# Last two row blocks of an attention and mixture-of-experts kernel: one due-time order for all operations, and W2's low parts by subtraction instead of an adding transfer

## The chip, the cores and the metric

One core of a Trainium2 chip runs the whole kernel. The metric is the device time of one execution in microseconds (us); the median of three runs of the kernel before is 937.79 us (935.74 to 939.01).

## The reference

Block-causal attention over 4 batches, 8 heads, 576 positions and 64 channels (mask block 64), and then a mixture of 4 experts whose weights are given row by row. All of it is float32.

```python
scores = scale * np.matmul(q, k.transpose(0, 1, 3, 2))       # masked where block_i < block_j
attn = softmax(scores)                                        # max, exp, sum
x = (attn @ v).transpose(0, 2, 1, 3).reshape(2304, 512)
p = domain_probs / (domain_probs.sum(-1, keepdims=True) + 1e-09)
for e in range(4):
    h = np.maximum(x @ w1[e], 0.0)                            # 512 -> 1024
    out += p[:, e:e+1] * (h @ w2[e])                          # 1024 -> 512
```

## The kernel before

**Precision.** TensorE gets every float32 operand as two parts: a high part, rounded by a copy to the type F32R, and a low part, the operand less its high part. A product is three matmuls (high by high, high by low, low by high). So each weight tile, each activation and each sum costs a copy (`a_copy`, line 407, ScalarE or VectorE, whichever would end first) and a subtraction (`tt` with SUB, line 413, VectorE) before TensorE can use it.

**Stages.** The 2304 rows are five blocks. Blocks 0, 1 and 2 go through the experts one at a time (`mm1`, `mm2`), beside the attention of the blocks that follow. The last 1024 rows, blocks 3 and 4, are taken together in `both_blocks` (line 1380), and there both layers use a scheme with 7 products of sub-blocks in place of 8 (Strassen's, in Winograd's form), which asks for sums and differences of sub-blocks of x, W1, h and W2, each split into parts again.

**The loop of `both_blocks`.** It runs over 16 pairs of F chunks, j = 0 to 15. A pair has 7 first-layer products (`product`, line 1588: 6 matmuls of 512 columns each). Between them stand second-layer units (`mm2_second`, line 1502: 3 matmuls of 256 columns each). Two pairs make a group g (7 groups); a group's 56 units run two pairs later, 28 in an even pair, by the shares `LATER[0] = [2, 4, 4, 4, 4, 5, 5]`, and 28 in the next, odd one, 4 after each product. TensorE's order is thus written out by hand. Within a group the units come by product x = 0 to 6 (the table `SECOND`: A11, S3, S2, A22, S1, A12, S4), each for the group's two pairs.

**What each group needs.** `w2_group` (line 1123), `w2_sums` (line 1137) and `w2_parts` (line 1151) make W2's parts: for each of the two pairs a quarter (x = 0, 256 columns) and three tiles of 512 columns (x = 1 to 3, two of them with sums of quarters). For x = 0 the low part is a VectorE subtraction. For x = 1 to 3 ScalarE writes the raw tile negated and rounded, which is minus the high part, into the low tile (line 1158), and GpSimd starts a transfer that adds the raw tile into it (`add_dma`, line 401). `h_group` (line 1427) and `h_parts` (line 1440) do the same split for h: 14 copies and 14 subtractions of 512 columns a group. `second_sums` (line 1450) makes the sums of h, `w_pair` (line 1100) those of W1, `snap` (line 1631) and `total` (line 1637) gather the first layer's products out of PSUM. `out_second` (line 1539) scales the finished second-layer tiles and, from the second group on, adds them to the output in DRAM by adding transfers of 128 KB on GpSimd's queue.

**Buffers.** Late in the kernel there are 6 tiles each for W2's high and low parts, 6 raw W2 tiles, 10 each for h's high and low parts, and 13 tiles `sc` for first-layer results and sums of h.

**What sets the order.** All of this is generated ahead of time by a planner, `Flow` (line 95). Every step is an `Op` with an engine, an estimated cost and a priority. `Flow.est` (line 135) estimates when each step could start; `Flow.run` (line 212) takes the earliest, and among the steps of the same engine that could start no later, the one with the lowest priority number. The result is a fixed instruction order on each engine; the engines work through it strictly in that order and wait for one another by semaphores. Before the change the priorities are fixed levels: 0.0 for what frees PSUM, 0.1 for sums of h, 0.2 or 0.4 for parts of h, 1.0 or 2.5 (5.0 when far off) for W1 and W2, 1.0 for output transfers. The planner also keeps GpSimd's steps, transfers among them, apart from VectorE's SBUF steps (`self.port`, lines 150 and 244).

Of the kernel before, what the change touches and what calls it, by code (L numbers as in the profile page):

```python
# [11 lines left out]
ALU = mybir.AluOpType  # L12
# [82 lines left out]
class Flow:  # L95
# [39 lines left out]
    def est(self, op):  # L135
        best = None
        for eng, cost in (op.eng if isinstance(op.eng, list) else [(op.eng, op.cost)]):
            t = self.clock[eng]
            for v in op.r:
                if v.t is None:  # L140
                    return None
                x = v.t + (self.SELF if v.eng == eng else self.LAT + op.lag + (self.SLACK if eng == "pe" else 0.0))
                if x > t:
                    t = x
            if op.bytes and len(self.landed) >= 8:
                t = max(t, self.landed[-8])
            for b in op.u:
                if b.base + self.LAT + op.lag / 2 > t:
                    t = b.base + self.LAT + op.lag / 2
            if eng == "pool":  # L150
                t = max(t, self.port)
            elif eng == "dve" and op.port:
                t = max(t, self.port)
                for a, b in self.held() if self.later else ():
                    if a - self.AHEAD < t < b:
                        t = b
            score = t + cost + self.bias.get(eng, 0.0) + (op.pen() if eng == "dve" else 0.0)
            if best is None or score < best[0]:
                best = (score, t, eng, cost)
        return best[1:]  # L160
# [51 lines left out]
    def run(self):  # L212
        while self.threads:
            k = 0
            while k < len(self.threads):
                th = self.threads[k]
                if self.advance(th):
                    k += 1
                else:
                    self.threads.pop(k)  # L220
            if not self.threads:
                break
            cands = []
            for th in self.threads:
                if isinstance(th[1], Op):
                    e = self.est(th[1])
                    if e is not None:
                        cands.append((e, th))
            assert cands, "stuck"
            first = min(cands, key=lambda c: (c[0][0], c[1][1].prio()))  # L230
            eng = first[0][1]
            near = [c for c in cands if c[0][1] == eng and c[0][0] <= first[0][0]]
            (t, eng, cost), th = min(near, key=lambda c: (c[1][1].prio(), c[0][0]))
            op = th[1]
            if eng == "pe" and self.fill:
                n = int((t - self.clock["pe"] - 700.0) / 216.0)
                for _ in range(n):
                    self.fill()
            op.fn(eng)
            if eng == "pe":  # L240
                cost *= self.pe
            end = t + cost
            self.clock[eng] = end
            if eng == "pool":
                self.port = t + (op.lock if self.later and op.lock else cost)
            elif eng == "dve" and op.port:
                self.port = end
            if op.bytes:
                arrive = max(end + op.wait, self.clock["dma"]) + op.bytes
                self.clock["dma"] = arrive  # L250
                end = arrive + 300.0
                self.landed.append(end)
            op.val.t, op.val.eng = end, eng
            for b in op.u:
                b.last = max(b.last, end)
            try:
                th[1] = th[0].send(op.val)
            except StopIteration:
                self.threads.remove(th)
# [3 lines left out]
def kernel(  # L263
# [10 lines left out]
    nc = tc.nc  # L274
# [125 lines left out]

    def add_dma(dst, src, nbytes, r, u, prio):

        o = op("pool", 1000.0, lambda _: nc.gpsimd.dma_start(out=dst, in_=src, accum_op=ALU.add), r, u, prio)
        o.bytes = nbytes / 180.0
        return o

# [635 lines left out]
    pairs = [(e, f) for e in range(E) for f in range(0, FC, 2)]  # L1042
    wt, hts, pns = {}, {}, {}

    def w_prio(i, which):
        i -= 4 * (i >= NC) * (which == 1)
        return lambda: (1.6 if i == 0 else 1.7 if i + which == 2 else 2.005) if now[0] == 0 else 1.0 if i <= now[0] + 1 else (2.5 if i <= now[0] + 2 else 5.0)

    def w_load(which, i, e, f):
        raw = yield fl.take(f"w{which}r")  # L1050
# [72 lines left out]
    def w2_group(g):  # L1123


        pr = lambda: 1.0 if now[0] >= NC + 4 * g + 2 else 2.5
        T = {}
        for j in (2 * g, 2 * g + 1):
            yield ("until", lambda: j in w2_raw)
            fl.spawn(w2_sums(j, T, pr))  # L1130
        for x in range(4):
            for j in (2 * g, 2 * g + 1):
                hi = yield fl.take("w2h", NC + 8 * g + 2 * x + j % 2)
                lo = yield fl.take("w2l", NC + 8 * g + 2 * x + j % 2)
                fl.spawn(w2_parts(j, x, hi, lo, T, pr))

    def w2_sums(j, T, pr):
        more, (r0, v0, _), (r1, v1, _) = w2_raw[j]
# [12 lines left out]
    def w2_parts(j, x, hi, lo, T, pr):  # L1151
        yield ("until", lambda: (j, x) in T)
        raw, deps, n = T[j, x]
        a = yield a_copy(hi.tile[:, :n], raw.tile[:, :n], n, deps, [raw, hi], pr)
        if x == 0:
            l = yield tt("dve", lo.tile[:, :n], raw.tile[:, :n], hi.tile[:, :n], SUB, n, deps + [a], [raw, hi, lo], pr)
        else:
            m = yield op("act", 0.833 * n + 95, lambda _: nc.scalar.activation(lo.tile, raw.tile, AF.Copy, scale=-1.0), deps, [raw, lo], pr)
            l = yield add_dma(lo.tile, raw.tile, P * n * 4, [m], [lo, raw], pr)
        w2s[j, x] = (hi, lo, a, l)  # L1160
        if x:
            if x == 1:
                yield ("until", lambda: (j, 2) in T)
            elif x == 3:
                yield ("until", lambda: (j, 2) in T)
            fl.give(raw)
# [134 lines left out]
    def prepare():  # L1301
# [37 lines left out]

        def split(x, src, deps, u):  # L1340
            hi, lo = xt[x]
            a = yield a_copy(hi.tile, src, n, deps, [hi, u], 0.5)
            l = yield tt("dve", lo.tile, src, hi.tile, SUB, n, deps + [a], [hi, lo, u], 0.5)
            xp[x] = (hi.tile, lo.tile, [a, l])
            return [a, l]

        got = yield from split("A22", a22, dv, x3)
        s1 = yield tt("dve", a22, a21, a22, ADD, n, dv + got, [x3], 0.5)
        s3 = yield tt("dve", a21, a11, a21, SUB, n, dv + [s1], [x2, x3], 0.5)
        yield from split("S3", a21, [s3], x3)  # L1350
        yield ("until", lambda: len(xready.get((PAIR, KC - 1), ())) == 2)
        old = [v for c in range(KC) for v in xready[PAIR, c]]
        s2 = yield tt("dve", a11, a22, a11, SUB, n, [s1, s3] + old, [x2, x3], 0.5)
        yield from split("S2", a11, [s2], x2)
        yield from split("S1", a22, [s1], x3)
        s4 = yield tt("dve", a12, a12, a11, SUB, n, [s2] + old, [x2], 0.5)
        yield from split("S4", a12, [s4], x2)
        for x, r in zip((x2, x3), XR):
            for k in range(KC):
# [20 lines left out]
    def both_blocks():  # L1380
# [14 lines left out]
        for j in range(len(pairs)):  # L1395
            now[0] = NC + 2 * j
            g = j // 2 - 1
            if j > 1:
                rest = [(g, x, jj, k) for x in range(7) for jj in (2 * g, 2 * g + 1) for k in range(4)][28 * (j % 2):][:28]
            st, banks = {}, {}  # L1400
            for (i, role), share in zip(*((CHAIN, LATER[j % 2]) if j > 1 else (CHAIN, SHARE) if j else (FIRST, SHARE1))):
                yield from product(j, i, role, banks, st)
                for _ in range(min(share, len(rest))):
                    x = rest.pop(0)
                    yield from (mm2(*x) if len(x) == 2 else mm2_second(*x))
            while rest:
                x = rest.pop(0)
                yield from (mm2(*x) if len(x) == 2 else mm2_second(*x))
# [31 lines left out]
    def h_parts(j, name, hh, hl, g, x):  # L1440
        b, deps, last = ha[j, name]
        n = MAXW
        pr = lambda: 0.2 if now[0] >= NC + 4 * g + 4 else 0.4
        a = yield a_copy(hh.tile[:, :n], b.tile[:, :n], n, deps, [b, hh], pr)
        l = yield tt("dve", hl.tile[:, :n], b.tile[:, :n], hh.tile[:, :n], SUB, n, deps + [a], [b, hh, hl], pr)
        hs[j, name] = (hh, hl, a, l)
# [92 lines left out]
    def out_second(g, x, k, bank, to, mm, done):  # L1539
# [6 lines left out]
        if what == "copy":  # L1546
# [4 lines left out]

            d = yield op("act", 0.833 * n + 95, fn, [mm, pns[bi]], [b], 0.0)
        else:
            b, d0 = sent.pop((g, t, k, half))
            d = yield op("dve", 1.04 * n + 130, lambda _: nc.vector.scalar_tensor_tensor(
                out=b.tile, in0=acc, scalar=pn, in1=b.tile, op0=MUL, op1=ADD), [mm, d0], [b], 0.0)
# [5 lines left out]
        dst = out[tok:tok + r, half * n:half * n + n]  # L1562
        if g:
            yield ("until", lambda: (bi, k, half) in part)
            v = yield add_dma(dst, b.tile[p0:p0 + r], r * n * 4, [d, part.pop((bi, k, half))], [b], 1.0)
        else:
            v = yield dma(dst, b.tile[p0:p0 + r], r * n * 4, [d], [b], 1.0)
        part[bi, k, half] = v
# [208 lines left out]
```

## Time and profile before

| | |
|---|---|
| median of 3 runs | 937.79 us |
| the profiled execution | 936.45 us |
| its span, first to last instruction | 934.7 us |
| TensorE busy / VectorE busy / ScalarE busy / GpSimd busy | 95% / 82% / 62% / 28% of the span |
| mean granted TensorE clock | 0.974 of full speed |

The span is 1.75 us shorter than the execution's own time. Engines in the rows: PE is TensorE, DVE VectorE, ACT ScalarE, POOL GpSimd, SP the queue of the plain loads. Times are us from the start of the span. A tile's trailing p in a row (`w2rp`, `hhp`) marks the tiles that were added late; tiles named `xh`, `xl` in rows of line 1523 are parts of h put into old buffers.

### The profile page before, as it was taken

The numbers are of one execution on the slowest core, as the hardware profiler recorded it, in microseconds if no ns is written. First come the engines' busy times: TensorE is split into PE (matmuls) and PEld (weight loads), VectorE is DVE, ScalarE is ACT, GpSimd is POOL, SyncE is SP. The second block draws the span as 40 slices with busy tenths as digits, with TensorE's granted clock in tenths as the row PEclk, the third lists the DMA queues.
The fourth block names the chain that finished last, engine by engine and source line by source line (L and its number), as shares of the span: only waits on it lengthen the run. The fifth ranks groups of instructions, "written<-read, shape, count | busy, mean of one in ns | idle before, by whom it ended". The sixth has DMA issues, their size and how long they took to land.

```text
span 934.7 us, 14450 instructions
## 1 busy us (share of the span) xinstructions
PE 886.7 (95%) x4907; PEld 738.9 (79%) x4907; DVE 763.8 (82%) x1385; ACT 575.5 (62%) x1222; POOL 261.9 (28%) x191
## 2 busy tenths in 40 slices
PE   8999999999999999999999998999798897969698
PEld 5877888878878878778788786899687786969687
DVE  6999999989899889989977999898677676767562
ACT  6787756756655646667446348676857566666640
POOL 1141101422322323224233301013434342526250
PEclk9999999999999999999999999899989798979899
DMA  7875487364354553564332315355676675858466
GB/s 180 212 197 163 130 205 197 85 157 109 95 148 89 129 139 102 146 154 101 95 102 79 90 46 136 100 160 108 108 146 102 125 124 113 136 113 109 95 74 197
DMA packets 236218, 119.10 MB, mean 127 GB/s; under 512 B 129008, under 2 KB 211184, under 8 KB 236144
## 3 DMA queue, kind: packets, MB, share of 16 engines
q1 hardware_dynamic: 215264, 94.05, 37.8%
q0 software_dynamic: 19872, 23.60, 17.7%
q8 instruction: 38, 0.62, 0.3%
q10 hardware_dynamic: 1008, 0.52, 0.2%
q14 instruction: 36, 0.29, 0.1%
HBM read 87.72 MB, written 19.40 MB: 115 GB/s over the span
## 4 chain that ended last, share of the span: by engine, by line
PE 87%; ACT 5%; DMA 3%; DVE 3%; SPq 2%; issue 1%; DVEq 0%; POOLq 0%
PE acc L1247 23%; PE h L1196 22%; PE acc L1523 14%; PE h L1614 9%; PE att L1614 7%; PE att L825 4%; PE acc L1683 2%; PE att L600 2%; PE att L599 2%; SPq L394 2%; DMA w2l<-w2rp 1%; DMA w2l<-w2r 1%; DMA probs_n<-in_moe_domain_probs_dram 1%; ACT xr L1634 1%; ACT ohp L1550 1%
## 5 line engine op out<-in xcount | busy, mean ns | idle before, releaser
L1196 PE MATMUL h<-xh,w1h 128*128 128x512 f32 (+1 forms) x384 | 137.0, 357 | 0.0
L1196 PE MATMUL h<-xh,w1l 128*128 128x512 f32 (+1 forms) x384 | 136.0, 354 | 0.0
L1196 PE MATMUL h<-xl,w1h 128*128 128x512 f32 (+1 forms) x384 | 135.8, 354 | 0.0
L750 POOL PARTITION_ALL_REDUCE sb<-sa x26 | 84.0, 3278 | 171.0 <-DVE tr L865 99.8
L1247 PE MATMUL acc<-w2h,hh 128*128 128x512 f32 x312 | 124.1, 398 | 0.0
L1247 PE MATMUL acc<-w2h,hl 128*128 128x512 f32 x312 | 121.8, 390 | 1.0 <-DVE hl L1216 1.0
L1247 PE MATMUL acc<-w2l,hh 128*128 128x512 f32 x312 | 121.8, 390 | 0.0
L771 POOL PARTITION_ALL_REDUCE mx<-cm x16 | 52.8, 3297 | 221.3 <-DVE cm L416 150.3
L409 ACT CAST w2h<-w2r 128x512 fp32r<-128x512 f32 (+1 forms) x113 | 69.1, 612 | 62.2 <-PE acc L1247 54.6
L416 DVE TENSOR_TENSOR w1l<-w1r,w1h 128x512 fp32r<-128x512 f32 (+1 forms) x128 | 88.9, 697 | 4.7 <-ACT w1h L409 4.0
L1214 ACT ACTIVATE hh<-h 128x512 fp32r<-128x512 f32 (+1 forms) x94 | 49.3, 525 | 68.1 <-PE h L1196 67.9
L409 ACT CAST w1h<-w1r 128x512 fp32r<-128x512 f32 (+1 forms) x113 | 68.9, 611 | 27.1 <-DMA w1r<-in_moe_w_dram 12.7
L1196 PEld LDWEIGHTS h<-xh,w1h 128*128 128x128 f32 x384 | 72.5, 189 | 11.3 <-issue 0.9
L1196 PEld LDWEIGHTS h<-xl,w1h 128*128 128x128 f32 x384 | 72.5, 189 | 10.3
L1196 PEld LDWEIGHTS h<-xh,w1l 128*128 128x128 f32 x384 | 72.4, 189 | 10.3
L416 DVE TENSOR_TENSOR w2l<-w2r,w2h 128x512 fp32r<-128x512 f32 (+1 forms) x102 | 70.6, 693 | 1.1 <-ACT w2h L409 0.8
L1247 PEld LDWEIGHTS acc<-w2h,hl 128*128 128x128 f32 x312 | 58.6, 188 | 14.3 <-DVE hl L1216 1.4
L1247 PEld LDWEIGHTS acc<-w2h,hh 128*128 128x128 f32 x312 | 58.7, 188 | 13.6 <-issue 1.2
L1247 PEld LDWEIGHTS acc<-w2l,hh 128*128 128x128 f32 x312 | 58.8, 188 | 9.8
L1216 DVE SCALAR_TENSOR_TENSOR hl<-h,hh 128x512 fp32r<-128x512 f32 (+1 forms) x94 | 55.6, 592 | 13.4 <-ACT hh L1214 12.8
L416 DVE TENSOR_TENSOR S<-S,mx 128x1024 f32<-128x1024 f32 (+4 forms) x80 | 59.7, 790 | 1.2 <-POOL mx L771 1.1
L727 ACT ACTIVATE S<-S 128x1024 f32<-128x1024 f32 (+4 forms) x80 | 55.4, 714 | 4.7 <-DVE S L416 4.5
(401 smaller groups left out, 2382.9 us busy)
## 6 DMA issues: line engine op xcount, KB each, us to landing
w1r<-in_moe_w_dram SPq DMA_DIRECT2D x120, 256.0 KB, 3.1
w2r<-in_moe_w_dram SPq DMA_DIRECT2D x113, 256.0 KB, 3.0
qr<-in_q_dram SPq DMA_DIRECT2D x112, 64.0 KB, 2.3
out_dram<-ohp POOLq DMA_DIRECT2D x48, 128.0 KB, 4.5
out_dram<-o POOLq DMA_DIRECT2D x48, 128.0 KB, 4.5
kr<-in_k_dram SPq DMA_DIRECT2D x64, 72.0 KB, 2.8
VN<-in_v_dram SPq DMA_DIRECT2D x32, 128.0 KB, 2.6
w2rp<-in_moe_w_dram SPq DMA_DIRECT2D x15, 256.0 KB, 3.5
```

The costliest lines, as they stand in the source:

```text
L409: o = op(engs, 0, lambda e: nc.scalar.copy(dst, src) if e == "act" else nc.vector.tensor_copy(dst, src), r, u, prio)
L416: o = op(engs, 0, lambda e: ENG[e].tensor_tensor(out=dst, in0=a, in1=b, op=alu), r, u, prio)
L727: exps.append((yield op("act", 0.833 * 2 * w + 95, lambda _: nc.scalar.activation(sv, sv, AF.Exp, scale=scale), [t], [Sb], pr)))
L750: sums.append((yield held(2300.0, op("pool", 150 + 6.3 * W, lambda _, h=h: nc.gpsimd.partition_all_reduce(sb.tile[:, h * W:h * W + W], sa. ...
L771: lambda _: nc.gpsimd.partition_all_reduce(mx.tile[:, :2 * W], src, P, RED.max),
L825: nc.tensor.matmul(out=x.tile[64 * g:64 * g + 64, W - w:W], lhsT=lhsT, rhs=rhs, start=(i == 0), stop=(i == len(todo) - 1))
L1196: nc.tensor.matmul(out=ps[:, :n], lhsT=s.tile[:, ks], rhs=x.tile[:, kc, :n], start=(kc == 0 and m == 0), stop=(kc == KC - 1 and m == 2),)
L1214: a = yield op("act", 0.833 * n + 55, lambda _: nc.scalar.activation(hh.tile[:, :n], ps[:, :n], AF.Relu), [mm], [pb, hh], 0.0)
L1216: l = yield op("dve", 1.04 * n + 70, lambda _: nc.vector.scalar_tensor_tensor(out=hl.tile[:, :n], in0=ps[:, :n], scalar=0.0, in1=hh.tile[: ...
L1247: nc.tensor.matmul(out=acc, lhsT=s.tile[:, ts], rhs=w.tile, start=(f == 0 and m == 0), stop=(f == FC - 1 and m == 2))
L1523: nc.tensor.matmul(out=acc[:, to], lhsT=s.tile[:, ts], rhs=v.tile[:, of], start=(start and first and m == 0 and k % 2 == 0), stop=(what != ...
L1614: nc.tensor.matmul(out=ps[:, :n], lhsT=w.tile[:, ks], rhs=x[:, kc, :n], start=(start and kc == 0 and m == 0), stop=(i in (2, 3, 4) and kc ...
```

## The change

All operations of `both_blocks` get priorities from one clock. `cur[0]` counts TensorE's progress: 3.5 a pair, 0.5 a product. A step needed at `at` has priority 0.05 plus 0.02 for each unit that `at` lies ahead. Parts of h are due at 7(g+1)+x, W2's parts at 7(g+1) + (0, 1, 2, 5), their sums at 7(g+1), the loads and splits of W1 and W2 of this stage at 1.75 per chunk. The sums of x go from 0.5 to 0.02, output transfers from 1.0 to 0.05. All W2 low parts are VectorE subtractions, so `add_dma` is left for the output alone. In the planner GpSimd's transfers no longer wait for VectorE's SBUF steps nor hold them off by `self.port`, and are estimated at 1400 ns instead of 1000. `out_second` lets the planner wait until the tile that it adds to exists.

```diff
             if eng == "pool":
-                t = max(t, self.port)
+                t = t if op.bytes else max(t, self.port)
...
-            if eng == "pool":
+            if eng == "pool" and not op.bytes:
                 self.port = t + (op.lock if self.later and op.lock else cost)
...
+    cur = [0.0]
+
+    def due(at):
+        return lambda: 0.05 + 0.02 * max(0.0, at - cur[0])
+
     def w_prio(i, which):
+        late_ = due((1.75 * (i - NC)) if which == 1 else 1.75 * (i - NC) + 7.0) if i >= NC else None
         i -= 4 * (i >= NC) * (which == 1)
-        return lambda: (1.6 if i == 0 else 1.7 if i + which == 2 else 2.005) if now[0] == 0 else 1.0 if i <= now[0] + 1 else (2.5 if i <= now[0] + 2 else 5.0)
+
+        def value():
+            if late_ and "sc" in fl.free:
+                return late_()
...
     def w2_group(g):
-        pr = lambda: 1.0 if now[0] >= NC + 4 * g + 2 else 2.5
+        pr = due(7.0 * (g + 1))
...
-                fl.spawn(w2_parts(j, x, hi, lo, T, pr))
+                fl.spawn(w2_parts(j, x, hi, lo, T, due(7.0 * (g + 1) + (0, 1, 2, 5)[x])))
...
-        if x == 0:
+        if x in (0, 1, 2, 3):
             l = yield tt("dve", lo.tile[:, :n], raw.tile[:, :n], hi.tile[:, :n], SUB, n, deps + [a], [raw, hi, lo], pr)
         else:
             m = yield op("act", 0.833 * n + 95, lambda _: nc.scalar.activation(lo.tile, raw.tile, AF.Copy, scale=-1.0), deps, [raw, lo], pr)
...
+            cur[0] = 3.5 * j
             for (i, role), share in zip(*((CHAIN, LATER[j % 2]) if j > 1 else (CHAIN, SHARE) if j else (FIRST, SHARE1))):
                 yield from product(j, i, role, banks, st)
+                cur[0] += 0.5
...
     def h_parts(j, name, hh, hl, g, x):
-        pr = lambda: 0.2 if now[0] >= NC + 4 * g + 4 else 0.4
+        pr = due(7.0 * (g + 1) + x)
...
     def out_second(g, x, k, bank, to, mm, done):
...
+            yield ("until", lambda: (g, t, k, half) in sent)
             b, d0 = sent.pop((g, t, k, half))
...
-            v = yield add_dma(dst, b.tile[p0:p0 + r], r * n * 4, [d, part.pop((bi, k, half))], [b], 1.0)
+            v = yield add_dma(dst, b.tile[p0:p0 + r], r * n * 4, [d, part.pop((bi, k, half))], [b], 0.05)
```

## Rows read from the trace of the kernel before

**Rows 1.** The page: span, and busy time of each engine.

```profile
span 934.7 us, 14450 instructions
PE 886.7 (95%) x4907; PEld 738.9 (79%) x4907; DVE 763.8 (82%) x1385; ACT 575.5 (62%) x1222; POOL 261.9 (28%) x191
```

**Rows 2.** Timeline, TensorE: first matmuls of pairs (start, length, line), and stage's end.

```profile
575.27 0.39 PE L1614 MATMUL att<-xh,w1h 128*128 128x512 f32 x1
...
642.62 0.40 PE L1614 MATMUL h<-xh,w1h 128*128 128x512 f32 x1
...
662.36 0.40 PE L1614 MATMUL att<-xh,w1h 128*128 128x512 f32 x1
...
691.12 0.40 PE L1614 MATMUL h<-xh,w1hp 128*128 128x512 f32 x1
...
909.02 0.50 PE L1683 MATMUL acc<-w2h,hhp 128*128 128x512 f32 x1 [0.21 <-ACT o L1550]
```

**Rows 3.** Timeline, TensorE: matmuls after a wait; in brackets idle time and releaser.

```profile
585.91 0.77 PE L1614 MATMUL att<-S2h,w1h 128*128 128x512 f32 x1 [5.59 <-DVE w1h L409]
...
675.41 0.38 PE L1523 MATMUL acc<-w2h,hhp 128*128 128x256 f32 x1 [3.05 <-ACT w2h L409]
...
679.57 0.58 PE L1523 MATMUL acc<-w2l,hhp 128*128 128x256 f32 x1 [3.78 <-DMA w2l<-w2rp]
```

**Rows 4.** Waits from 600 to 900 us: total, times, longest; TensorE's in second layer.

```profile
PE acc L1523 <- ACT w2h L409: 16.6, 5, 3.4
...
PE acc L1523 <- DMA w2l<-w2rp: 11.4, 3, 3.8
...
PE acc L1523 <- DMA w2l<-w2r: 7.3, 2, 3.7
```

**Rows 5.** Timeline, VectorE, ahead of the wait at 672 us.

```profile
658.97 0.41 DVE L416 TENSOR_TENSOR w2rp<-w2rp 128x256 f32<-128x256 f32 x1
...
663.95 0.69 DVE L416 TENSOR_TENSOR hl<-xr,hh 128x512 fp32r<-128x512 f32 x1 [3.23 <-ACT hh L409]
...
667.32 0.68 DVE L416 TENSOR_TENSOR hl<-xr,hh 128x512 fp32r<-128x512 f32 x1
667.92 0.69 DVE L416 TENSOR_TENSOR xl<-scp,xh 128x512 fp32r<-128x512 f32 x1
...
674.28 0.42 DVE L416 TENSOR_TENSOR w2rp<-w2rp,w2r 128x256 f32<-128x256 f32 x1
```

**Rows 6.** Timeline, other engines, same stretch: a load, ScalarE's two steps, GpSimd's issue.

```profile
639.94 0.37 SPq L394 DMA_DIRECT2D w2r<-in_moe_w_dram  x1
...
674.74 0.62 ACT L409 CAST w2h<-w2rp 128x512 fp32r<-128x512 f32 x1
675.26 0.63 ACT L1158 ACTIVATE w2l<-w2rp 128x512 fp32r<-128x512 f32 x1
...
676.18 0.86 POOL L403 DMA_DIRECT2D w2l<-w2rp  x1 [11.82 <-DVE w2rp L416]
```

**Rows 7.** Windows, one group each: length, busy PE, PEld, DVE, ACT, POOL, clock, DMA.

```profile
626.50:675.41 48.91, 45.86 (x296) 41.55 (x294) 37.93 (x74) 37.61 (x78) 16.74 (x19) 1.00 0.59 108
675.41:724.25 48.84, 41.67 (x253) 37.39 (x253) 35.56 (x72) 32.42 (x66) 19.45 (x22) 0.93 0.69 119
...
823.11:873.05 49.94, 42.88 (x252) 38.46 (x253) 34.26 (x69) 31.61 (x64) 19.48 (x22) 0.90 0.67 111
```

**Rows 8.** Windows, short ones: into the stage, the first wait, a later wait.

```profile
540.00:550.00 10.00, 10.00 (x46) 8.29 (x45) 10.00 (x14) 3.15 (x5) 0.00 (x0) 1.00 0.18 52
...
580.50:586.00 5.50, 0.09 (x1) 0.12 (x1) 5.40 (x11) 3.86 (x8) 0.86 (x1) 0.84 0.04 8
...
720.00:729.00 9.00, 1.97 (x10) 1.47 (x9) 5.68 (x13) 6.92 (x14) 3.98 (x6) 0.73 0.29 37
729.00:739.00 10.00, 10.00 (x49) 8.95 (x48) 4.27 (x8) 5.35 (x11) 1.34 (x2) 0.73 0.95 206
```

**Rows 9.** DMA issues from 560 to 900 us: count, size, median us to landing.

```profile
w2l<-w2rp POOLq DMA_DIRECT2D x15, 256.0 KB, 4.1
```

More of the change, by code (lines that the diff above doesn't have):

```diff
@@ L401, in add_dma @@
     def add_dma(dst, src, nbytes, r, u, prio):
-        o = op("pool", 1000.0, lambda _: nc.gpsimd.dma_start(out=dst, in_=src, accum_op=ALU.add), r, u, prio)
+        o = op("pool", 1400.0, lambda _: nc.gpsimd.dma_start(out=dst, in_=src, accum_op=ALU.add), r, u, prio)
         o.bytes = nbytes / 180.0
@@ L1043 @@
     wt, hts, pns = {}, {}, {}
+    cur = [0.0]
+    def due(at):
+        return lambda: 0.05 + 0.02 * max(0.0, at - cur[0])
     def w_prio(i, which):
+        late_ = due((1.75 * (i - NC)) if which == 1 else 1.75 * (i - NC) + 7.0) if i >= NC else None
         i -= 4 * (i >= NC) * (which == 1)
-        return lambda: (1.6 if i == 0 else 1.7 if i + which == 2 else 2.005) if now[0] == 0 else 1.0 if i <= now[0] + 1 else (2.5 if i <= now[0] + 2 else 5.0)
+        def value():
+            if late_ and "sc" in fl.free:
+                return late_()
+            if now[0] == 0:
+                return 1.6 if i == 0 else 1.7 if i + which == 2 else 2.005
+            return 1.0 if i <= now[0] + 1 else 2.5 if i <= now[0] + 2 else 5.0
+        return value
     def w_load(which, i, e, f):
@@ L1341, in split @@
             hi, lo = xt[x]
-            a = yield a_copy(hi.tile, src, n, deps, [hi, u], 0.5)
-            l = yield tt("dve", lo.tile, src, hi.tile, SUB, n, deps + [a], [hi, lo, u], 0.5)
+            a = yield a_copy(hi.tile, src, n, deps, [hi, u], 0.02)
+            l = yield tt("dve", lo.tile, src, hi.tile, SUB, n, deps + [a], [hi, lo, u], 0.02)
             xp[x] = (hi.tile, lo.tile, [a, l])
@@ L1347, in prepare @@
         got = yield from split("A22", a22, dv, x3)
-        s1 = yield tt("dve", a22, a21, a22, ADD, n, dv + got, [x3], 0.5)
-        s3 = yield tt("dve", a21, a11, a21, SUB, n, dv + [s1], [x2, x3], 0.5)
+        s1 = yield tt("dve", a22, a21, a22, ADD, n, dv + got, [x3], 0.02)
+        s3 = yield tt("dve", a21, a11, a21, SUB, n, dv + [s1], [x2, x3], 0.02)
         yield from split("S3", a21, [s3], x3)
@@ L1352, in prepare @@
         old = [v for c in range(KC) for v in xready[PAIR, c]]
-        s2 = yield tt("dve", a11, a22, a11, SUB, n, [s1, s3] + old, [x2, x3], 0.5)
+        s2 = yield tt("dve", a11, a22, a11, SUB, n, [s1, s3] + old, [x2, x3], 0.02)
         yield from split("S2", a11, [s2], x2)
         yield from split("S1", a22, [s1], x3)
-        s4 = yield tt("dve", a12, a12, a11, SUB, n, [s2] + old, [x2], 0.5)
+        s4 = yield tt("dve", a12, a12, a11, SUB, n, [s2] + old, [x2], 0.02)
         yield from split("S4", a12, [s4], x2)
```

## The prediction

> **What bounds the kernel now.** I read the page first: TensorE is busy 95% of the span, VectorE 82% [rows 1]. So the kernel is TensorE's, and what can be won is TensorE's idle time and the time that it runs at the lower clock. Next the timeline of TensorE through the stage that the diff touches. The reader is to see two kinds of pair. From 642.62 to 662.36 a pair takes 19.74 us; the next, with the same kind of work (7 products, 28 units), takes from 662.36 to 691.12, 28.76 us [rows 2]. One step, a product with four units, is thus 19.74/7 = 2.82 us, and an undisturbed group of two pairs 39.48 us. From 662.36 to the stage's end at 909.02 there are 246.66 us for five groups, whose work is 5 x 39.48 = 197.40: 49.26 us are lost. From 575.27 to 662.36, the first two groups, 87.09 us against 78.96: 8.13 lost. Together 57.4 us, and this is all that an order can bring.
>
> Where they are lost, the matmuls after a wait show: one of 5.59 us at 580 for a W1 copy on VectorE, and then the pattern of 675.41 and 679.57, 3.05 us for the high part of a W2 tile from ScalarE and 3.78 us for the transfer that makes its low part [rows 3]. The view of waits says that the pattern stands five times, once a group: 16.6 us for the high part, 11.4 + 7.3 = 18.7 us for the transfer [rows 4]. That is 35.3 of the 49.3 us. [...]
>
> Why the W2 tile is late, the timelines of the other engines show. It is a tile of W2 sums for the unit S3 of the group's second pair. Its raw data was asked for at 639.94 [rows 6]. Its first sum ran at 658.97, and the next, which needs only that and raw data, at 674.28, 15 us later [rows 5], with TensorE already waiting since 672.4. Between them VectorE waited 3.23 us for ScalarE and then worked on parts of h without a break worth speaking of. Parts of h have 0.2 or 0.4 and W2 has 1.0 or more, so eleven of a group's fourteen splits of h, which become possible all at once at the end of an odd pair, go ahead of a W2 tile that is needed sooner than most of them: S3 of the second pair is the group's 13th unit, 672; A12 and S4, the last parts of h, are needed 20 us and more after it.
>
> **The change part by part.** *Order.* By the new numbers the W2 tile of that unit is due one unit of the clock into the group, the parts of h for A22 to S4 three to six. So the sum at 674.28 would go right behind 659.4, 13 us before TensorE comes to it; its copy and low part cost 0.62 and 0.69. I take it that all five waits go, and with them the stretches at the lower clock: 49.3 us. The lower bound is a half of it, if the 3.4 us for the high part stay (first rival).
>
> *Low parts on VectorE.* Six a group (three tiles, two pairs), 42 in all. VectorE's like instructions start 0.60 us apart (667.32, 667.92 [rows 5]): 3.6 us a group, 25.2 us in all. Removed are 42 ScalarE steps of 0.62 to 0.63 us and 42 GpSimd issues of 0.86 us [rows 6] with their transfers, which took 4.1 us to land [rows 9]. On the path that is the gain even with an unchanged order: now 679.57 - 674.28 = 5.3 us from sum to TensorE, then sum, copy and low part, about 1.8 us. VectorE is busy 34.3 to 35.6 us in a group of 49 to 50 us now [rows 7]; with 3.6 more it is 38 to 39 us in a group that shall take 39.48. Those busy times count isolated instructions at 0.69 us that start 0.60 us apart when queued, so there is some more room, but this is the change's cost: cover almost without slack. Into the stage it has none already: VectorE is busy 10.00 of 10.00 us from 540 to 550, and 5.40 of 5.50 in TensorE's first wait [rows 8]. The bounds of what the 25.2 us bring back are 0 (all hidden under TensorE) and 25.2 (none hidden). The windows of 1.00 clock show a group at 37.93 busy in 48.91 us with only the first 3 us of a wait in it [rows 7], nearer to hidden; I take a quarter, 6.3 us.
>
> *First groups.* The 8.1 us around 580 are VectorE's backlog, most of it parts of h that the new order puts behind W1, but up to six low parts come on top. Bounds 0 and 8.1 us gained, taken 4.1.
>
> *Waits and queues.* Each low part on VectorE now waits for ScalarE's copy of the same tile, and everything behind it on VectorE waits too; such a wait is 3.23 us at worst in these rows [rows 5], and it comes where ScalarE has a backlog. ScalarE gets 42 x 0.62 = 26 us lighter, which speaks for fewer of them, so no term of its own. GpSimd's queue then holds only the output's adding transfers, which no longer stand behind a W2 issue that waits, as for 11.82 us at 676.18 [rows 6]; 96 x 0.86 = 83 us of issues over six groups of 39.5 us: hidden, and without that cover still only the last four would count, 3.4 us. W1 and W2 loads on the SP queue move up by due time; a raw tile comes free at VectorE's read instead of at a landing, so they can only be asked for sooner. The planner's own lines (the port, 1400 ns, the wait for a tile's existence) issue nothing; they only shift the order.
>
> *Sum.* -49.3 - 4.1 + 6.3 = -47.1 us. Against the profiled execution (936.45, span 934.7): 889.4. The runs' median is 1.3 us higher, so 937.8 - 47.1 = 890.7, given as 891.
>
> **The rivals.** *Waits remain, shorter.* VectorE at 38 of 39.5 us has no room for its own waits, and TensorE waits for it a little in each group. If the wait for the high part stays (3.4 us, with half of a group's clock loss, 1.4) in five groups, 24 us come back: 914. The same comes out if all 25.2 us of low parts show and the first groups gain nothing: 937.8 - 49.3 + 25.2 = 914. For it: the full windows of [rows 8]. Against: the deadlines are loose, see above. TensorE's clock belongs here: a wait of 7 us is followed by 0.73 over ten microseconds [rows 8]; whether several short waits would do it too, no row shows. [...]
>
> *Slower: first-layer results hold their buffers.* Place: `snap`, which takes a tile `sc`; there are 13. At the end of an odd pair the two pairs' results and sums hold 10, and the next pair asks for 6. Until now parts of h come first and free them at once. By due time the parts of S1, A12 and S4 may be left until four to six units into the group; then `snap` finds no tile, PSUM isn't freed, and the next product waits. Price: a product held back until such a part is due waits up to four steps, 4 x 2.82 = 11.3 us, in seven groups 79 us, less the 53.4 recovered: 964. It decides from 53.4/7 = 7.6 us a group. For it: VectorE's small slack, which keeps parts from being done early. Against: S3 and A22 come due first and free four tiles, and VectorE takes whatever is ready when nothing is due.
>
> *The order hardly changes.* Priorities decide only among steps that could start no later than the earliest one; if the planner's estimates leave few such choices, the waits for the high part stay and only the transfer's part goes: five times 3.7 less 0.7 us, 15 us, against 6 to 25 us on VectorE: 929 to 948. Against: 15 us between two sums of which the second was ready [rows 5] can't come from estimates alone.
>
> **How the numbers follow.** The forecast, 878 to 903, has 0.60; shorter waits, 903 to 930, 0.20; an order that hardly changes 0.07; slower by the buffers 0.11; 0.02 for better than 878 (all 57.4 us gained would be 880). The range 878 to 930 holds the first two. About 0.3% (2.8 us) is what a measurement of this kernel can tell from no change. Faster by more: 0.82; within: 0.06; slower: 0.12.
>
> **What would show it.** In the profile after: no wait of TensorE on a W2 tile over 1 us from 600 to 900, no transfer into `w2l` at all, even pairs near 19.7 us, groups near 39.5 to 41 us, a mean clock of 0.99 or more, VectorE busy 37 to 38 us of each group, and the stage's end some 47 us sooner. The order step is wrong if the sums of W2 still stand behind parts of h; the price of the low parts is wrong if VectorE's windows are full and TensorE waits for low parts; the slower rival is right if products wait for `snap` or `total` in each group. The prediction falls if groups stay over 45 us.

## The result, and the profile after

The changed kernel takes 880.65 us (median of 4 runs, 880.60 to 882.55) against 937.91 us (4 runs, 935.74 to 939.01). The ratio is 0.9397 with a 95% interval of 0.9376 to 0.9418: 57.3 us less, inside the range of 878 to 930 and 10 us below the 891 forecast. The mean granted TensorE clock is 0.999, before 0.974.

The page after, against [rows 1]: span, busy time of each engine, granted clock in 40 slices.

```profile
span 878.8 us, 14341 instructions
PE 870.3 (99%) x4905; PEld 726.7 (83%) x4907; DVE 785.6 (89%) x1443; ACT 542.5 (62%) x1164; POOL 224.8 (26%) x149
...
PEclk9999999999999999999999999999999999999999
```

The span is 55.9 us shorter. VectorE does more (785.6 us against 763.8) in less time, and GpSimd has the 42 issues less (149 instructions, 191 before). The timeline of TensorE, first matmuls of pairs, against [rows 2]:

```profile
576.29 0.39 PE L1631 MATMUL att<-xh,w1h 128*128 128x512 f32 x1
...
635.66 0.40 PE L1631 MATMUL h<-xh,w1h 128*128 128x512 f32 x1
...
655.40 0.40 PE L1631 MATMUL att<-xh,w1h 128*128 128x512 f32 x1
...
694.88 0.40 PE L1631 MATMUL att<-xh,w1h 128*128 128x512 f32 x1
...
853.17 0.50 PE L1700 MATMUL acc<-w2h,hhp 128*128 128x512 f32 x1 [0.21 <-ACT o L1566]
```

The pair from 635.66 to 655.40 takes the 19.74 us that an undisturbed pair took before, and the group from 655.40 to 694.88 takes 39.48 us. The seven groups from 576.29 to 853.17 take 276.88 us; 7 x 39.48 are 276.36. Of the 57.4 us lost in them before, 0.5 are left. The stage ends 55.85 us sooner (853.17 against 909.02), the other 1.0 us being that its third pair starts at 576.29 and not at 575.27. From 550 us to the end the view of waits has one single row for TensorE, against [rows 4]:

```profile
PE acc L1700 <- ACT o L1566: 0.2, 1, 0.2
```

So every wait of [rows 3] is gone, the one near 580 us among them. Windows of two groups (length, busy PE, PEld, DVE, ACT, POOL, clock, DMA), against [rows 7]:

```profile
655.40:694.90 39.50, 39.50 (x255) 35.90 (x254) 38.29 (x79) 26.46 (x55) 14.13 (x16) 1.00 0.65 108
694.90:734.50 39.60, 39.60 (x255) 36.01 (x254) 38.39 (x80) 26.56 (x55) 14.14 (x16) 1.00 0.65 107
```

TensorE is never idle and VectorE is busy 38.3 of 39.5 us. And the W2 tile that was late, in the timelines of VectorE and ScalarE, against [rows 5] and [rows 6]:

```profile
642.41 0.42 DVE L416 TENSOR_TENSOR w2r<-w2r 128x256 f32<-128x256 f32 x1
...
643.08 0.42 DVE L416 TENSOR_TENSOR w2r<-w2r,w2r 128x256 f32<-128x256 f32 x1
...
644.32 0.62 ACT L409 CAST w2h<-w2r 128x512 fp32r<-128x512 f32 x1 [0.40 <-PE acc L1539]
...
648.59 0.68 DVE L416 TENSOR_TENSOR w2l<-w2r,w2h 128x512 fp32r<-128x512 f32 x1
```

Its second sum runs at 643.08, 12.3 us before its group's first product (655.40). Before, it ran at 674.28, 11.9 us behind that product (662.36). Relative to TensorE it moved 24 us.

### The profile page after: what moved, and what is told of

It is laid out like the page before. It is cut to its first block, busy times and chain, and to the rows that moved or that the text cites. A ratio compares the mean times of both kernels' runs of the same rounds, so it can differ in the third digit from the quotient of the medians.

```text
span 878.8 us, 14341 instructions
## 1 busy us (share of the span) xinstructions
PE 870.3 (99%) x4905; PEld 726.7 (83%) x4907; DVE 785.6 (89%) x1443; ACT 542.5 (62%) x1164; POOL 224.8 (26%) x149
## 4 chain that ended last, share of the span: by engine, by line
PE 94%; DMA 2%; SPq 2%; ACT 1%; DVE 1%; issue 0%; DVEq 0%; ACTq 0%
PE acc L1261 24%; PE h L1210 24%; PE acc L1539 16%; PE h L1631 10%; PE att L1631 8%; PE att L825 5%; PE acc L1700 3%; PE att L600 2%; PE att L599 2%; SPq L394 2%; DMA w2r<-in_moe_w_dram 1%; PE acc L587 0%; DMA w1r<-in_moe_w_dram 0%; PE acc L825 0%; DMA S<-in_k_dram 0%
## 5 line engine op out<-in xcount | busy, mean ns | idle before, releaser
L1228 ACT ACTIVATE hh<-h 128x512 fp32r<-128x512 f32 (+1 forms) x94 | 49.3, 524 | 64.4 <-PE h L1210 64.1
L403 POOL DMA_DIRECT2D out_dram<-ohp x48 | 42.6, 1394 | 161.1 <-DVE ohp L1572 161.1
L416 DVE TENSOR_TENSOR w2l<-w2r,w2h 128x512 fp32r<-128x512 f32 (+1 forms) x112 | 77.1, 689 | 0.9 <-ACT w2h L409 0.8
L403 POOL DMA_DIRECT2D out_dram<-o x48 | 42.4, 1382 | 76.7 <-DVE o L1572 63.4
```

Of the source, the lines that this page charges most:

```text
L403: o = op("pool", 1400.0, lambda _: nc.gpsimd.dma_start(out=dst, in_=src, accum_op=ALU.add), r, u, prio)
L416: o = op(engs, 0, lambda e: ENG[e].tensor_tensor(out=dst, in0=a, in1=b, op=alu), r, u, prio)
L1228: a = yield op("act", 0.833 * n + 55, lambda _: nc.scalar.activation(hh.tile[:, :n], ps[:, :n], AF.Relu), [mm], [pb, hh], 0.0)
```

## The experiments

The change has three parts that can be taken apart: the planner's lines for GpSimd's transfers, the due numbers, and the low parts by VectorE. The first question was whether the order or the transfers had made the waits.

**e1, the changed kernel with transfers back.**

```diff
-        if x in (0, 1, 2, 3):
+        if x == 0:
```

> The changed kernel with the adding transfers back for W2's three tiles per pair (x = 1 to 3); order by due time as changed. Theory (the waits came from the order, W2's sums stood 15 us behind parts of h): with the sum 13 us early a transfer that lands 4 us later is hidden as well, so TensorE's waits are gone and the time is 880 to 888 us. Rival (the waits came from the transfers, which also hold the raw tiles until they land): 3.7 us a group and the clock behind it stay, 905 to 920 us.

Measured: 880.76 us (ratio 0.9405, 0.9386 to 0.9423), the same as the whole change; TensorE's only wait in the stage:

```profile
PE acc L1700 <- ACT o L1566: 0.3, 1, 0.3
```

The rival falls: started as early as in this order, the transfers cost nothing here (880.76 against 880.65 us). And under the new order the low parts on VectorE bring nothing and cost nothing.

**e2, the kernel before with all low parts by VectorE.**

```diff
-        if x == 0:
+        if x in (0, 1, 2, 3):
```

> The kernel before with one edit: W2's low parts all by VectorE; order as before. Theory: the high part still comes late from ScalarE, 3.4 us in each of five groups, and 3.6 us a group more on VectorE lengthen the backlog ahead of it; only the transfer's 3.7 us less 0.7 go: 920 to 940 us. Rival (transfers are the cause): 890 to 905 us.

Measured: 945.21 us, ratio 1.0086 (1.0071 to 1.0101): 0.9% slower than before, 5 us above what the theory expected. Two of TensorE's waits (timeline, idle time and releaser in brackets); two such waits, of 1.8 to 5.5 us, stand in each of five groups:

```profile
729.16 0.58 PE L1523 MATMUL acc<-w2l,xh 128*128 128x256 f32 x1 [3.83 <-DVE w2l L416]
...
741.81 0.58 PE L1523 MATMUL acc<-w2lp,xh 128*128 128x256 f32 x1 [4.43 <-DVE w2lp L416]
```

The group's two old waits, for the high part from ScalarE and for the transfer (35.3 us in all), are gone; in their place stand two for low parts on VectorE (37.8 us in all). The sentence that the removed transfer is a gain "even with an unchanged order" is wrong.

**e4, the changed kernel with parts of h ahead of all else.** This tests the cause that the prediction named.

```diff
-        pr = due(7.0 * (g + 1) + x)
+        pr = lambda: 0.01
```

> The changed kernel with parts of h at priority 0.01, ahead of everything but the freeing of PSUM, all else by due time. Theory: W2's sums stand behind parts of h again and a wait of 3 to 4 us for the high part comes back in most groups, with the clock's loss behind it: 900 to 925 us. Rival (it is the numbers for W1, W2 loads and transfers that matter, not h against W2): 880 to 884 us.

Measured: 881.03 us (ratio 0.9396, 0.9382 to 0.9410). Nothing comes back. The late tile's sums and the group's first product (timelines):

```profile
648.73 0.42 DVE L416 TENSOR_TENSOR w2r<-w2r 128x256 f32<-128x256 f32 x1
...
652.09 0.42 DVE L416 TENSOR_TENSOR w2r<-w2r,w2r 128x256 f32<-128x256 f32 x1
...
656.07 0.40 PE L1631 MATMUL att<-xh,w1h 128*128 128x512 f32 x1
```

The second sum is still 4.0 us ahead of the product, though every part of h ranks before it. So in the changed kernel parts of h can rank first without making W2 late, and the expected return of the wait is refuted.

**e3, the changed kernel with the planner's three old lines.**

```diff
-                t = t if op.bytes else max(t, self.port)
+                t = max(t, self.port)
...
-            if eng == "pool" and not op.bytes:
+            if eng == "pool":
...
-        o = op("pool", 1400.0, ...
+        o = op("pool", 1000.0, ...
```

> The changed kernel with the planner's three old lines: GpSimd's transfers kept apart from VectorE's SBUF steps, 1000 ns an issue. Theory: the output's transfers are off the path, so their place in the order moves nothing: 879 to 883 us. Rival: freeing GpSimd's issues was what let VectorE's order become dense, and 5 to 20 us come back: 886 to 900 us.

Measured: 919.67 us, ratio 0.9812 (0.9788 to 0.9835): 39.0 of the 57.3 us are lost again, twice what the rival had allowed. This is the miss that settled the matter. The timeline of one group, and a window behind its first wait:

```profile
655.91 0.42 DVE L416 TENSOR_TENSOR w2r<-w2r,w2r 128x256 f32<-128x256 f32 x1
...
656.47 0.40 PE L1631 MATMUL att<-xh,w1h 128*128 128x512 f32 x1
...
754.14 0.48 PE L1539 MATMUL acc<-w2hp,xl 128*128 128x256 f32 x1 [2.71 <-DVE xl L416]
...
760.49 0.38 PE L1539 MATMUL acc<-w2h,hhp 128*128 128x256 f32 x1 [1.95 <-ACT hhp L409]
```

```profile
754.10:770.00 15.90, 13.68 (x63) 11.74 (x64) 13.80 (x27) 10.16 (x23) 0.00 (x0) 0.79 0.16 51
```

The due numbers did what they say: the W2 sum is 0.6 us ahead of the product, not 11.9 behind, and TensorE waits for no W2 tile. Instead it waits for parts of h, in four of the five groups for 2.71 and 1.95 us, and in the window read it runs at a mean clock of 0.79 behind it. Its waits in the five groups add up to 21.7 us. Due numbers without the planner's lines choose who is late; with the low parts on VectorE they gain 18 of the 57 us.

**New theory, and f1, the planner's lines alone in the kernel before.** In the plan each GpSimd transfer held VectorE's SBUF steps off for its whole issue, 22 of them a group [rows 7], 1 us each. Old priorities and old transfers stay. This run, like f2 and h1, also has the change's line in `out_second` that waits until a tile exists; no run takes that line apart, nor the 1400 ns.

```diff
-                t = max(t, self.port)
+                t = t if op.bytes else max(t, self.port)
...
-            if eng == "pool":
+            if eng == "pool" and not op.bytes:
...
-        o = op("pool", 1000.0, ...
+        o = op("pool", 1400.0, ...
```

> The kernel before with the planner's lines on GpSimd's transfers alone (no longer kept apart from VectorE's SBUF steps, 1400 ns), old priorities, W2's low parts by transfers as before. New theory (the planner let some 22 issues a group block VectorE for 1 us each, so its idea of when VectorE is free, and with it the order, was wrong; the due numbers matter little): the five waits of 7 us go, the first wait near 580 us may stay as with W1's old levels: 881 to 895 us. Old theory (W2 stands behind parts of h by its priority, whatever the planner thinks of the port): 915 to 938 us.

Measured: 888.48 us, ratio 0.9477 (0.9455 to 0.9499): 48.7 us of gain from lines that issue no instruction. The late tile's second sum, two more sums of the same pair, the group's first product, one of TensorE's five waits:

```profile
647.97 0.42 DVE L416 TENSOR_TENSOR w2rp<-w2rp,w2r 128x256 f32<-128x256 f32 x1
648.31 0.42 DVE L416 TENSOR_TENSOR w2rp<-w2r,w2rp 128x256 f32<-128x256 f32 x1
...
665.45 0.42 DVE L416 TENSOR_TENSOR w2rp<-w2r,w2rp 128x256 f32<-128x256 f32 x1
...
655.53 0.40 PE L1615 MATMUL att<-xh,w1h 128*128 128x512 f32 x1
...
672.62 0.38 PE L1523 MATMUL acc<-w2l,hh 128*128 128x256 f32 x1 [1.34 <-DMA w2l<-w2rp]
```

With W2 at 1.0 and more and parts of h at 0.2 and 0.4, the second sum runs 7.6 us ahead of the product. What is left is a wait of 1.2 to 1.5 us for a transfer in each of five groups. It hangs on the pair's fourth sum, which still runs 9.9 us behind the first product (665.45) and 17 us behind its last input (648.31), with nine splits of h between them: the lag that the prediction saw is still there in part, at 6.6 us of waiting in all. And the first wait near 580 us, which the expectation let stand, is gone too, without a single due number: the third to sixth pair take 78.94 us (576.59 to 655.53).

**f2, the same with the low parts by VectorE.** The edit of e2 on top of f1.

> The same with W2's low parts all by VectorE as well; old priorities. New theory: as without the low parts, 881 to 895 us, the low parts being covered or not by old priorities: a few us more than with transfers. Old theory: W2's parts late by priority, with VectorE fuller, 915 to 945 us. Together with the other three corners this tells what low parts cost under old priorities.

Measured: 901.68 us, ratio 0.9614 (0.9600 to 0.9628), 7 us above the range and 13.2 us above f1. The first of its waits:

```profile
588.59 0.77 PE L1615 MATMUL att<-S2h,w1h 128*128 128x512 f32 x1 [6.45 <-DVE w1h L409]
```

Under old priorities the fuller VectorE makes W1 late in the first groups (6.45 us) and W2's low parts in the later ones (8.3 us in five waits). Here the due numbers earn their place: with them the low parts are covered (880.65), without them they cost 13 us.

**g1 and g2, the changed kernel with one planner line back each.** g1: a transfer waits in the plan until VectorE leaves the port. g2: a transfer holds VectorE's SBUF steps off.

```diff
-                t = t if op.bytes else max(t, self.port)
+                t = max(t, self.port)
```

> The changed kernel with one planner line back: a GpSimd transfer waits in the plan until VectorE's SBUF steps leave the port, but doesn't hold them off. New theory: only the holding off matters; here the issues come later in GpSimd's own queue, which has room: 880 to 885 us. Rival: this is the line that costs the 39 us: 905 to 920 us.

```diff
-            if eng == "pool" and not op.bytes:
+            if eng == "pool":
```

> The changed kernel with the other planner line back: each of the output's 16 transfers a group holds off VectorE's SBUF steps in the plan for its 1400 ns, 22 us of each 39.5. New theory: this line costs what both cost together, 900 to 925 us. Rival: it is harmless alone, 880 to 885 us.

Measured: g1 880.95 us (ratio 0.9394, 0.9372 to 0.9416), nothing lost. g2 929.04 us (ratio 0.9905, 0.9888 to 0.9923): 48.4 us lost by one condition, a little more than expected. One of its waits:

```profile
764.17 0.55 PE L1539 MATMUL acc<-w2hp,xl 128*128 128x256 f32 x1 [3.65 <-DVE xl L416]
```

g2 holds off for 1400 ns a transfer, e3 for 1000 (with the other line as well), and they lose 48.4 and 39.0 us.

**e7, the changed kernel with old levels for W1's and W2's loads and splits.**

```diff
-            if late_ and "sc" in fl.free:
-                return late_()
```

> The changed kernel with W1's and W2's loads and splits of this stage at their old levels (1.0, 2.5, 5.0); sums and parts of W2, parts of h and sums of x by due time. Theory: the first groups' loss, 5.6 us of waiting for a W1 copy near 580 us and 2.5 us of the clock, comes back, since W1 stands behind parts of h again: 886 to 895 us; if W1 waits in each pair, more, up to 920. Rival (the first wait came from the sums of x or from W2): 880 to 883 us.

Measured: 887.75 us, ratio 0.9470 (0.9456 to 0.9484): 7.1 us back, as expected, in one wait and the lower clock around it (0.73 from 573.7 to 583.0):

```profile
573.71 0.77 PE L1629 MATMUL h<-S2h,w1h 128*128 128x512 f32 x1 [4.55 <-DVE w1h L409]
```

The place and the reason are not the expected ones. The wait stands in the second pair, ahead of the seven groups, which lose nothing here; before, it stood in the third. And what goes ahead of W1 is W2: from 556 to 570.8 us VectorE runs 14 sums and low parts of W2, which have due numbers, and not one step of W1, whose next sum starts at 570.80; in the changed kernel the same sum starts at 556.40.

**h1, the kernel before with only the holding off removed and W1's and W2's loads and splits by due time.** g2's line as in the change, and the new `w_prio` with its clock.

> The kernel before with two pieces of the change only: transfers no longer hold off VectorE in the plan, and W1's and W2's loads and splits of this stage by due time. Low parts by transfers, W2's sums and parts of h, sums of x and output transfers at old priorities. Without the due numbers for W1 and W2 the one planner change gave 888 us, with five waits of 1.3 us for W2's transfers. If W1's and W2's loads by due time are what is left: 880 to 883 us. If those five waits come from the old priorities of W2's sums and parts: 886 to 890 us.

Measured: 894.00 us, ratio 0.9537 (0.9515 to 0.9559), above both expectations. The five waits of f1 are gone, but two new ones stand in the third pair, with a clock of 0.72 behind them (592 to 609 us):

```profile
592.44 0.58 PE L1539 MATMUL acc<-w2h,hh 128*128 128x256 f32 x1 [5.64 <-ACT w2h L409]
...
597.23 0.58 PE L1539 MATMUL acc<-w2l,hh 128*128 128x256 f32 x1 [4.21 <-DMA w2l<-w2rp]
```

With W1's and W2's loads and splits ahead and W2's sums still at 1.0 and more, these sums (590.84 and 591.31) come last in VectorE's backlog of the third pair, while TensorE waits from 586.8. So a due time for some of the steps can make others late. That it is worse than for none (f1, 888.5) is not shown, because h1 also keeps the planner's old line of g1 and the 1000 ns; which of the rest is needed was not taken further apart.

**e5 and e6, the cover and the buffers.** e5 computes each W2 low part twice; e6 has 11 tiles `sc` in place of 13.

```diff
             l = yield tt("dve", lo.tile[:, :n], raw.tile[:, :n], hi.tile[:, :n], SUB, n, deps + [a], [raw, hi, lo], pr)
+            l = yield tt("dve", lo.tile[:, :n], raw.tile[:, :n], hi.tile[:, :n], SUB, n, deps + [a, l], [raw, hi, lo], pr)
```

> The changed kernel with each W2 low part computed twice on VectorE, one after the other: 4.3 us a group more (six of 0.60, two of 0.34). It measures the cover of the low parts. If VectorE's 38 us of a 39.5 us group leave only 1.5 us, the surplus of some 2.8 us in each of seven groups shows: 895 to 905 us. If the cover is larger (instructions in a queue start 0.60 us apart, not 0.69), 881 to 886 us.

```diff
-        add("sc", 5, [P, MAXW])
+        add("sc", 3, [P, MAXW])
```

> The changed kernel with 11 tiles sc instead of 13, a test of the rival that first-layer results hold their buffers. If the due order leaves parts of h until they are due, the buffers are near their limit and two fewer cost waits of products for a step or more, 2.8 us in each of seven groups: 900 us or more. If the parts are made early all the same, 880 to 884 us.

Measured: e5 902.65 us (ratio 0.9628, 0.9614 to 0.9642), 22.0 us more than the change, so the cover doesn't hold this much more work. How far it reaches, the run doesn't measure. TensorE's waits add up to 12.5 us, the rest goes with a clock of 0.993 in the mean; the loss is uneven (the group from 787.82 to 827.30 takes 39.48 us, the one before it 45.97); and the planner moved copies to ScalarE (19 instructions more), so that VectorE is busy for 21.7 us more and not for 7 x 4.3 = 30. TensorE's first two rows of waits in e5 are for parts of h, released by their copies on ScalarE:

```profile
PE acc L1540 <- ACT hhp L409: 4.7, 3, 2.3
PE acc L1540 <- ACT xh L409: 4.1, 3, 2.3
```

e6 881.86 us (ratio 0.9407, 0.9393 to 0.9421): 1.2 us for two buffers, and no wait of TensorE in the groups. The 13 are not near a limit.

All corners that were run, in us (the new planner lines with `out_second`'s wait for a tile, which e3 has as well):

| | low parts by transfers | low parts by VectorE |
|---|---|---|
| old planner lines, old priorities | 937.9 (before) | 945.2 (e2) |
| new planner lines, old priorities | 888.5 (f1) | 901.7 (f2) |
| old planner lines, due numbers | not run | 919.7 (e3) |
| new planner lines, due numbers | 880.8 (e1) | 880.65 (the change) |

## Why the prediction was right, and where it was not

*Where the time could come from.* Right: 57.4 us were counted as lost in the seven groups, and 57.3 us came off the median. All waits and all stretches at the lower clock went together, as the sum for the five groups had it (49.3 us; 246.66 less 197.77 are 48.9). But that the time came out inside the range is luck as far as the reason goes: the change carried the planner's lines along with the order. The range, 878 to 930, would have held e3 (919.67) and g2 (929.04) too, in which due numbers and low parts stand as the prediction argued them and most of the gain is lost.

*Why the W2 tile was late.* Wrong as the cause of the lost time, though the rows were read rightly. The step that failed is "Parts of h have 0.2 or 0.4 and W2 has 1.0 or more, so [they] go ahead". Under the old planner lines the ranks decide only which tile comes late: with due numbers it is parts of h in place of W2 (e3), and 39 of the 57 us stay lost. Under the new lines e4 gives parts of h the first rank and loses nothing; f1 leaves the old ranks and has the second sum 19.5 us earlier relative to TensorE (7.6 us ahead of the product in place of 11.9 behind). What was left to all the due numbers together is the 8 us from f1 to e1. Priorities only choose among steps that the planner believes could start; that sentence stood in the third rival and was not followed to its end.

*The planner's own lines.* This is the sentence that cost the reason: they "issue nothing; they only shift the order". The order that they shift is worth 48.7 us alone (f1), and one of them loses 48.4 us when taken back alone (g2). I had priced them at nothing because no instruction hangs on them; the title doesn't name them either. That this condition makes the difference is shown: g2 has it alone, and g1, the other line alone, loses nothing. How a plan with VectorE blocked by each issue leads to an order that the chip then waits in is argued from the code; no run shows the steps from the wrong estimate to the wrong order. The planner's other way of keeping VectorE off GpSimd's steps, `held`, was left as it is and was not tested.

*The low parts.* The work was sized rightly (38 to 39 us of VectorE foreseen in a group, 38.3 measured), the charge was not: a quarter of 25.2, 6.3 us, taken; -0.1 us measured (change against e1). The quarter was a guess between bounds, and the window that it leaned on is no single group: 626.50 to 675.41 holds 296 matmuls, a group 253. Nor did VectorE get all of the 42 subtractions on top: against e1 it has 25 instructions and 15.6 us more, because the planner moved copies to ScalarE. Where the edge lies, e5 doesn't measure. But the cover holds only with the due numbers: 13.2 us without them (f2 against f1), 7.5 us in the kernel before.

*The first groups.* Taken at 4.1 of 8.1 us, measured nearly all: the third to sixth pair take 655.40 - 576.29 = 79.11 us against 78.96. Half of it was too careful. Why it came, the forecast had wrong as well: f1 loses nothing in these pairs (78.94 us) without any due number, so the planner's lines alone remove the wait near 580 us. Without due numbers for W1 and W2, W1 comes late where the other steps have them (7.1 us, e7) or where VectorE has the low parts (6.45 us of waiting in f2). These two terms, 6.3 and 4.0, are the 10 us between 891 and 880.65.

*The rivals.* Shorter waits: not in the changed kernel, but e3 is what they look like. Buffers: refuted by e6. An order that hardly changes: no. On the clock, the first rival left open whether several short waits lower it as well. Its 1.4 us, half of a group's clock loss, are half of (49.3 - 35.3)/5, an estimate: no run shows the term by itself, and what the runs show in its place are the clocks behind single waits. The changed kernel has no idles to test it on; f1, f2 and e3 have some, and they differ. Around f1's single wait of 1.34 us the window from 671 to 685 keeps 1.00; behind f2's single wait of 3.30 us (675.13) the clock is 0.80; behind e3's 2.71 us with 1.95 us following it is 0.79, and in e3's first group, with waits of only 1.06 and 1.25 us close together, it falls to 0.62 for a while. The windows of f1, f2 and of that group of e3:

```profile
671.00:685.00 14.00, 12.66 (x84) 11.43 (x83) 11.73 (x26) 7.63 (x16) 4.16 (x6) 1.00 0.72 137
...
675.10:690.60 15.50, 15.47 (x83) 14.11 (x84) 12.27 (x23) 8.45 (x17) 0.00 (x0) 0.80 0.35 103
...
668.00:672.00 4.00, 2.75 (x9) 2.34 (x9) 4.00 (x9) 3.33 (x8) 0.00 (x0) 0.62 0.00 0
```

So one wait of 1.3 us a group costs little more than itself here (clock 1.00), one of 3.3 us has a lower clock behind it as well (0.80), and so have two short ones close together (0.62 from 668 to 672). Many short idles in a row no run here has by themselves.

## What to carry to other kernels

Where an order comes out of a planner, look for the resources in its model before its priorities: a conflict that it believes in and the traces don't show moves whole chains, and no instruction shows it. A tile that is late although its inputs were ready raises the question when the planner thought the engine free. And take the parts of a change apart before naming one of them as the cause: here the planner's lines were worth 49 us (f1), the due numbers 8 on top of them (f1 to e1), and the low parts on VectorE nothing or a loss, depending on the other two.

## What the runs showed of the hardware

In the rows read, GpSimd's issues and VectorE didn't hold one another off. Four issues, VectorE's copy of a float32 SBUF tile in the midst of them, and the window of just these 3.53 us, in the changed kernel:

```profile
683.86 3.53 POOL L403 DMA_DIRECT2D out_dram<-ohp  x4 [2.11 <-DVE ohp L1572]
...
685.59 0.42 DVE L409 CAST w1h<-w1r 128x512 fp32r<-128x512 f32 x1
```

```profile
683.86:687.39 3.53, 3.53 (x23) 3.14 (x22) 3.53 (x9) 1.15 (x2) 3.53 (x4) 1.00 0.91 140
```

The issues take 3.53 us, 0.88 us an issue, with VectorE busy for all of that time. Four others in the same trace take 3.53 us with VectorE idle throughout, and four in the kernel before, at 645.70, took 3.54 us with VectorE busy for 2.94 of them:

```profile
853.05:856.58 3.53, 3.41 (x15) 2.71 (x16) 0.00 (x0) 0.80 (x3) 3.53 (x4) 1.00 0.67 75
...
645.70:649.24 3.54, 3.54 (x23) 3.15 (x22) 2.94 (x8) 1.73 (x4) 3.54 (x4) 1.00 0.62 66
```

VectorE's copy and subtractions keep their 0.42 and 0.68 us. Nor did the copy delay the issues: 3.53 us with it among VectorE's steps, and 3.53 us with VectorE idle. The output's transfers landed at a median of 4.0 and 4.3 us after their issue, 4.5 before; the four at 683.86 and the four at 853.05 at 4.0 and 4.1 us.
